# Mixing the last 64 tokens of two batches together, on the two column halves of the TensorE array

## Chip, cores and metric

The kernel runs on one core of one Trainium2 chip. The metric is device time in microseconds (us), lower is better; faster or slower needs 2%. PE is TensorE (PEld its weight loads), DVE is VectorE, ACT is ScalarE, POOL is GpSimd. "The page" is the printed profile of a run, and its chain is the work that ended last, followed back from the last instruction.

## The reference, cut

```python
# attention over pooled keys and values: 8 batches, 8 heads, 576 tokens, head width 64
k_p, v_p = means of k, v over groups of 8 tokens
x = softmax(q @ k_p^T / 8) @ v_p             # -> [8, 576, 512] float32
# residual MLP with a token mix
a1  = alpha1 * x + beta1
tok = einsum('ts,bsd->btd', w_tok, a1)       # mixes the 576 tokens of one batch
u   = x + lam * tok
ch  = relu((alpha2 * u + beta2) @ w_ch1) @ w_ch2
out = u + lam * ch
```

576 tokens are four chunks of 128 and a remainder of 64. The mix contracts 576 source tokens in five steps (four of 128, one of 64 or 65 with a bias row) for each chunk of target tokens.

## The kernel before, the parts concerned

The remainders of an even batch and of the odd one after it share one chunk of 128 rows: the even batch's tokens in rows 0 to 63, the odd batch's in rows 64 to 127. Each was mixed in its own batch's turn, with a full-width matmul of which half the rows were used.

```python
def chunk_of(b, c):
    key = (b, c) if c < 4 else (b - b % 2, 4)      # remainders of a pair: one chunk
    ...                                            # (cut) makes u (f32) and u_bf (bf16)

def mix_T(b, c, eng=nc.vector):
    key, s = chunk_of(b, c)
    p0, p1 = (0, P) if c < 4 else (64 * (b % 2), 64 * (b % 2) + 64)
    xs = xs_pool[b % 2]
    ps_tok = gp("ps_tok")
    t0 = P * c - 64 * (b % 2) if c == 4 else P * c
    for sc in range(5):
        kk, at = (P, sc) if sc < 4 else (P, 5) if b % 2 else (65, 4)
        nc.tensor.matmul(out=ps_tok, lhsT=wtT[0:kk, at, t0:t0 + P],          # L512
                         rhs=xs[0:kk, sc, :], start=(sc == 0), stop=(sc == 4))
    nc.vector.tensor_tensor(out=s["u"][p0:p1, :], in0=st1[b]["x"][p0:p1, c, :],
                            in1=ps_tok[p0:p1, 0:DM], op=ALU.add)             # L514
    eng.tensor_tensor(out=s["u_bf"][p0:p1, :], in0=s["u"][p0:p1, :],
                      in1=al2_bc[p0:p1, :], op=ALU.mult)                     # L516

def mix_uT(key):      # four PE transposes of u_bf (L527), one ACT copy into u_fm (L529)
    ...               # (cut)
```

The program is a list of pieces per block, sorted by a hand-chosen place. Block n runs the MLP of four chunks (`mlp_A` at places 0 to 15: matmuls L543 and a ReLU on ACT, L548; `mlp_B` at 16 to 31: matmuls L566) and in between the attention and the mix of batch n + 1.

```python
for c in range(5):
    at = 25.2 + 0.8 * c if late else 24.6 + (0.9 if b % 2 else 1.0) * c     # late: b == 1
    todo.append((at, lambda c=c: mix_T(b, c)))
    if c < 4 or b % 2:
        key = (b, c) if c < 4 else (b - 1, 4)
        todo.append((at + 2.2, lambda key=key: mix_uT(key)))
...                                                   # (cut)
if n == 0:
    todo.append((12.6, lambda: mix_T(0, 4)))
...                                                   # (cut) and, at the kernel's start:
keep_warm(4)                                          # four matmuls of constants, unused
```

The softmax here doesn't subtract the row's maximum and nothing guards it: scores larger than these inputs give would overflow.

Of the kernel before, what the change touches and what calls it, by code (L numbers as in the profile page):

```python
# [7 lines left out]
FP = mybir.dt.float32  # L8
F16 = mybir.dt.float16
BF = mybir.dt.bfloat16  # L10
AF = mybir.ActivationFunctionType
ALU = mybir.AluOpType
AX = mybir.AxisListType

P = 128
SPG = 72
DM = 512
# [6 lines left out]
def kernel(  # L24
# [18 lines left out]
    nc = tc.nc  # L43
    ctx.enter_context(tc.manual_schedule())
    B, H, S, D = q.shape

    const = ctx.enter_context(tc.tile_pool(name="const", bufs=1))
    work = ctx.enter_context(tc.tile_pool(name="work", bufs=1))
# [3 lines left out]
    def gp(name):  # L52
        return psA.tile([P, 512], FP, tag="gp", name=name)
# [10 lines left out]
    def keep_warm(count):  # L64

        ps = gp("ps_warm")
        for _ in range(count):
            nc.tensor.matmul(out=ps, lhsT=warm[:, 0:P], rhs=warm)


    st1 = {}

    def new_batch(b):
        st1[b] = {"qT": {}, "ET": [None] * H, "raw": [None] * 2, "q": [None] * 2,
                  "k": [None] * 2, "v": [None] * 2}
# [57 lines left out]
    def sum_k(b, u, eng):  # L133

        t = st1[b]["raw"][u][:, 1]
        bf = work.tile([P, 2, 2, D], BF, tag="k_bf", bufs=4, name="k_bf")
        for n in (4, 2):
            eng.tensor_tensor(out=t[:, :, 0:n], in0=t[:, :, 0:n], in1=t[:, :, n:2 * n], op=ALU.add)  # L138
        eng.tensor_tensor(out=bf, in0=t[:, :, 0:1].to_broadcast((P, 2, 2, D)),
                          in1=t[:, :, 1:2].to_broadcast((P, 2, 2, D)), op=ALU.add)  # L140
        st1[b]["k"][u] = bf
# [11 lines left out]
    al2_bc = const.tile([P, DM], FP, tag="al2_bc", name="al2_bc")  # L153
# [9 lines left out]
    start = const.tile([1, 2], FP, tag="start", name="start")  # L163
# [54 lines left out]
    def consts(shape, dt, name, count):  # L218
        return [const.tile(shape, dt, tag=f"{name}_{i}", name=f"{name}_{i}") for i in range(count)]
# [5 lines left out]
    xs_pool = consts([P, 5, DM], BF, "xs", 2)  # L225
# [3 lines left out]
    wtT = const.tile([P, 6, 640], BF, tag="wtT", name="wtT")  # L229

    def fill_v(i):
        nc.vector.memset(vp1_pool[i][0][0:64], 8.0)
        nc.vector.memset(vp1_pool[i][1][0:64], 0.0)
        nc.vector.memset(vp1_pool[i][1][64:128], 8.0)
        nc.vector.memset(vrem_pool[i][64:128], 0.0)
        nc.vector.memset(vrem_pool[i][0:64], 8.0)
# [27 lines left out]
    def broadcast(i):  # L264

        ps = psB.tile([P, DM], FP, tag="ch", bufs=2, name="ps_bc")
        nc.tensor.matmul(out=ps, lhsT=ones_row, rhs=vecs[0:1, i])
        return ps
# [226 lines left out]
    def chunk_of(b, c):  # L495
        key = (b, c) if c < 4 else (b - b % 2, 4)
        if key not in st2:
            st2[key] = {
                "u": work.tile([P, DM], FP, tag="u_sb", bufs=12, name="u_sb"),
                "u_bf": work.tile([P, DM], BF, tag="u_bf", bufs=4, name="u_bf"),  # L500
            }
        return key, st2[key]

    def mix_T(b, c, eng=nc.vector):
        key, s = chunk_of(b, c)
        p0, p1 = (0, P) if c < 4 else (64 * (b % 2), 64 * (b % 2) + 64)
        xs = xs_pool[b % 2]
        ps_tok = gp("ps_tok")
        t0 = P * c - 64 * (b % 2) if c == 4 else P * c
        for sc in range(5):  # L510
            kk, at = (P, sc) if sc < 4 else (P, 5) if b % 2 else (65, 4)
            nc.tensor.matmul(out=ps_tok, lhsT=wtT[0:kk, at, t0:t0 + P],  # L512
                             rhs=xs[0:kk, sc, :], start=(sc == 0), stop=(sc == 4))
        nc.vector.tensor_tensor(out=s["u"][p0:p1, :], in0=st1[b]["x"][p0:p1, c, :],  # L514
                                in1=ps_tok[p0:p1, 0:DM], op=ALU.add)
        eng.tensor_tensor(out=s["u_bf"][p0:p1, :], in0=s["u"][p0:p1, :],  # L516
                          in1=al2_bc[p0:p1, :], op=ALU.mult)

    def mix_uT(key):
        s = st2[key]  # L520
# [60 lines left out]


    new_batch(1)
    keep_warm(4)
    ps_lam = broadcast(0)
    nc.scalar.copy(out=lam_bc, in_=ps_lam)
    ps_lamal = broadcast(1)
# [73 lines left out]
        mlp_A(0, j, 256, 512)  # L661
    fill_v(1)

    ticks = const.tile([1, 2], FP, tag="ticks", name="ticks")

    def tick():
# [7 lines left out]
    def attention(b):  # L674


        late = b == 1
        todo = [(0.55 if late else -2.0, lambda: cast_rem(b, nc.gpsimd)),
                (10.0 if late else 6.0, lambda: sum_v_rem(b, nc.gpsimd)),
                (12.4 if late else 11.6, lambda: att_Vrem(b, nc.scalar.copy))]  # L680
        for u in range(2):
            copy = nc.scalar.copy if late and u else nc.gpsimd.tensor_copy
            q_at, f_at, k_at, v_at = (((0.5, 3.6, 5.4, 9.5), (6.0, 8.2, 10.0, 11.6))[u] if late else
                                      (None, 2.7 + 6.6 * u, 5.5 + 6.6 * u, 4.2 + 6.6 * u))
            k_from = q_at + 0.1 if late else -1.0 + u
            if late:
                todo.append((q_at, lambda u=u, copy=copy: cast_q(b, u, copy)))
            todo.append((k_from, lambda u=u: sum_k(b, u, nc.gpsimd)))
            todo.append((f_at, lambda u=u: att_F(b, u)))
            todo.append((f_at + 0.1, lambda u=u: att_Frem(b, (u,), nc.scalar.copy)))  # L690
            todo.append((k_at, lambda u=u: att_K(b, u, nc.vector.tensor_copy)))
            todo.append((v_at, lambda u=u: sum_v(b, u)))
            todo.append((v_at + (1.6 if late else 3.4 - u), lambda u=u: att_V(b, u, nc.scalar.copy)))
        for h in range(8):
            at = 13.3 + 1.0 * h if late else 13.1 + 1.0 * h
            todo.append((at, lambda h=h: att_S(b, h)))
            todo.append((at + 2.0, lambda h=h: att_AV(b, h)))
            if h % 2:
                eng = nc.vector if h == 7 else nc.gpsimd
                todo.append((at + 2.1, lambda h=h, eng=eng: att_X(b, h - 1, h + 1, eng)))  # L700
        todo.append((29.4, tick))
        if b > 1:
            todo.append((-2.1, pool_wait))
        for c in range(5):
            at = 25.2 + 0.8 * c if late else 24.6 + (0.9 if b % 2 else 1.0) * c
            todo.append((at, lambda c=c: mix_T(b, c)))
            if c < 4 or b % 2:
                key = (b, c) if c < 4 else (b - 1, 4)
                todo.append((at + 2.2, lambda key=key: mix_uT(key)))
        return todo  # L710

    for n in range(NBLK):
        todo = []
        for j in range(0 if n else 4, NJ):
            todo.append((j, lambda j=j: mlp_A(n, j)))
        for m in range(4):
            for part in range(4):
                at = 16 + (4 * m + part if n else 4 * part + m)
                todo.append((at, lambda m=m, part=part: mlp_B(n, m, part)))
        if n == 0:  # L720
            todo.append((12.6, lambda: mix_T(0, 4)))
            todo.append((13.0, lambda: row_of_xs(1, nc.gpsimd)))
            todo.append((9.4, lambda: setup_wtok(4, nc.scalar.copy)))
            todo.append((10.8, lambda: setup_rowsum(4)))
            todo.append((24.2, setup_wtok_odd))
            for g in range(1, 4):
                todo.append((4 * g - 0.8, lambda g=g: setup_bias(g)))
            for g in range(4):
                todo.append((3.0 + 1.5 * g, lambda g=g: load_w2(g)))
        if n == NBLK - 2:  # L730
            for j in range(NJ):
                todo.append((0.5 + 1.5 * j, lambda j=j: scale_w2(j)))
        b = n + 1
        if b < B:
            todo += attention(b)
            if b + 1 < B:
                new_batch(b + 1)
                for u in range(2):
                    todo.append((28.7 + 1.5 * u, lambda b=b, u=u: cast_q(b + 1, u, nc.scalar.copy)))
                    at = 21.0 + 0.2 * u if b == 1 else 0.4 + 1.0 * u  # L740
                    todo.append((at, lambda b=b, u=u: load_qk(b + 1, u)))
                    at = 23.0 + 0.2 * u if b == 1 else 5.8 + 6.6 * u
                    todo.append((at, lambda b=b, u=u: load_v(b + 1, u)))
                todo.append((21.1 if b == 1 else 0.9, lambda b=b: load_rem(b + 1)))
                todo.append((23.1 if b == 1 else 6.0, lambda b=b: load_v_rem(b + 1)))
        for _, do in sorted(todo, key=lambda x: x[0]):
            do()
# [30 lines left out]
```

## Time and profile before

| | before |
|---|---|
| median (first three runs) | 369.9 us (369.81 to 370.09) |
| span of the profiled run | 368.9 us |
| PE busy; share of the chain | 97%; 94% |
| first token mix to end of span | 368.95 - 25.60 = 343.35 us |

The prediction below shows the rows on PE and on the mix. One more view: ACT in block 0, from the timeline of the kernel before (columns: start, length in us, engine, line, operation, tiles, forms, count; in brackets the idle time before and who ended it).

```profile
39.57 0.69 ACT L548 ACTIVATE Hj<-ps_h,bias_cols 128x512 bf16<-128x512 f32 x1 [0.32 <-PE ps_h L543]
40.16 1.04 ACT L130 CAST q_bf<-qk_raw 128x1024 bf16<-128x1024 f32 x1
...
48.04 0.75 ACT L444 CAST vp<-ps_v 8x264 f16<-8x264 f32 x2
49.34 0.69 ACT L548 ACTIVATE Hj<-ps_h,bias_cols 128x512 bf16<-128x512 f32 x1 [0.55 <-PE ps_h L543]
```

ACT has one gap of 0.32 us before 39.57 and one of 0.55 us before 49.34. Two more, of 0.44 us before 45.81 and 0.21 us before 47.33, are the same in both kernels; otherwise, up to 55 us, it works without a break.

### The profile page before, as it was taken

What the parts mean: (1) busy time and instruction counts of PE and PEld (TensorE: products, weight loads), DVE (VectorE), ACT (ScalarE), POOL (GpSimd) and SP (SyncE); (2) the same over time, 40 slices, a digit from 0 to 9 for tenths busy, and PEclk for the clock granted to TensorE, in tenths of its full rate; (3) what the DMA queues carried; (4) which work ended last, traced back from release to release, by engine and by line L of the source; (5) the groups of instructions that cost most, each with busy time, mean ns of one, the idle gap of its engine ahead of it and who ended that gap; (6) DMA issues with size and microseconds to landing.
All of it is one profiled execution on the core that took longest, in us unless ns stands there. A gap on an engine that the chain in (4) does not pass through costs nothing.

```text
span 368.9 us, 6184 instructions
## 1 busy us (share of the span) xinstructions
PE 359.0 (97%) x2346; PEld 197.7 (54%) x2346; DVE 220.4 (60%) x437; ACT 213.9 (58%) x420; POOL 126.3 (34%) x182
## 2 busy tenths in 40 slices
PE   7799999999999999999999999999999999999995
PEld 2477555555545554555455555555455545544544
DVE  8765554883786358744876387727863687543011
ACT  3765984389527970698148923895279705712710
POOL 8766914072507231542227140905072410000000
PEclk9999999999999999999999999999999999999999
DMA  7999994039102901183107502470100002002002
GB/s 251 254 217 308 245 279 160 14 121 340 54 34 83 338 24 55 57 292 93 59 28 235 181 30 57 150 265 30 53 32 2 29 31 57 2 28 85 2 28 85
DMA packets 19575, 43.27 MB, mean 117 GB/s; under 512 B 2193, under 2 KB 4565, under 8 KB 19546
## 3 DMA queue, kind: packets, MB, share of 16 engines
q1 hardware_dynamic: 17488, 37.89, 30.8%
q0 software_dynamic: 1888, 4.86, 7.1%
q8 instruction: 18, 0.29, 0.3%
q10 hardware_dynamic: 170, 0.14, 0.2%
q14 instruction: 11, 0.09, 0.1%
HBM read 38.30 MB, written 9.44 MB: 129 GB/s over the span
## 4 chain that ended last, share of the span: by engine, by line
PE 94%; ACT 2%; DVE 2%; DMA 1%; ACTq 0%; issue 0%; DVEq 0%
PE ps_ch L566 34%; PE ps_h L543 33%; PE ps_tok L512 12%; PE ps_sc L453 5%; PE ps_av L470 2%; PE ps_uT L527 2%; PE ps_q L369 2%; DMA vecs<-in_moe_alpha_dram 1%; ACT Hj L548 1%; PE ps_w L288 1%; PE ps_av L473 1%; PE ps_rs L300 0%; PE ps_kp L401 0%; DVE qk_raw L138 0%; DVE xs L273 0%; ACT u_fm L529 0%
## 5 line engine op out<-in xcount | busy, mean ns | idle before, releaser
L543 PE MATMUL ps_h<-u_fm,w 128*128 128x512 bf16 (+1 forms) x592 | 134.7, 373 | 0.6 <-ACT u_fm L529 0.4
L566 PE MATMUL ps_ch<-w,Hj 128*128 128x512 bf16 x512 | 127.2, 379 | 0.0
L548 ACT ACTIVATE Hj<-ps_h,bias_cols 128x512 bf16<-128x512 f32 x144 | 97.1, 691 | 34.1 <-PE ps_h L543 33.6
L543 PEld LDWEIGHTS <-w 128*128 128x128 bf16 x592 | 64.1, 114 | 48.2 <-issue 0.6
L566 PEld LDWEIGHTS <-Hj 128*128 128x128 bf16 x592 | 55.6, 98 | 49.1 <-issue 0.2
L529 ACT COPY u_fm<-ps_uT 128x512 bf16<-128x512 bf16 x36 | 21.0, 588 | 80.4 <-PE ps_uT L527 80.4
L484 POOL TENSOR_TENSOR xs<-x_tm,lamal_bc 128x512 bf16<-128x512 f32 x24 | 30.5, 1272 | 81.2 <-DVE x_tm L477 81.2
L455 ACT ACTIVATE ET<-ps_sc 128x288 f16<-128x288 f32 (+1 forms) x128 | 51.6, 488 | 10.8 <-PE ps_sc L453 10.4
L512 PE MATMUL ps_tok<-xs,wtT 128*128 128x512 bf16 (+1 forms) x200 | 49.3, 379 | 0.0
L573 DVE TENSOR_TENSOR u_sb<-u_sb,ps_ch 128x512 f32<-128x512 f32 (+1 forms) x37 | 24.9, 672 | 24.9 <-PE ps_ch L566 23.8
L408 DVE CAST kpT<-ps_kp 64x288 bf16<-64x288 f32 x31 | 14.1, 455 | 40.6 <-PE ps_kp L404 40.4
L572 DVE TENSOR_TENSOR ps_ch<-lam_bc,ps_ch 128x512 f32<-128x512 f32 x32 | 22.2, 693 | 24.9 <-PE ps_ch L566 24.8
L514 DVE TENSOR_TENSOR u_sb<-x_tm,ps_tok 128x512 f32<-128x512 f32 (+1 forms) x40 | 27.4, 685 | 12.0 <-PE ps_tok L512 11.9
L477 DVE TENSOR_TENSOR x_tm<-ps_av,rec 128x320 f32<-128x320 f32 x64 | 31.5, 492 | 2.7
L475 DVE RECIPROCAL rec<-ps_av 128x5 f32<-128x5 f32 x64 | 12.4, 193 | 34.4 <-PE ps_av L473 34.2
L512 PEld LDWEIGHTS <-wtT 128*128 128x128 bf16 (+1 forms) x200 | 18.8, 98 | 23.3 <-DVE xs L484 1.9
L453 PE MATMUL ps_sc<-qT,kpT 128*128 128x288 bf16 (+1 forms) x128 | 29.1, 306 | 1.5 <-DVE kpT L408 1.5
L138 POOL TENSOR_TENSOR qk_raw<-qk_raw 128x512 f32<-128x512 f32 (+1 forms) x28 | 29.9, 1068 | 1.1
L516 DVE TENSOR_TENSOR u_bf<-u_sb,al_bc 128x512 bf16<-128x512 f32 (+1 forms) x39 | 27.3, 700 | 1.4
L671 POOL COPY ticks<-ticks 1x1 f32<-1x1 f32 x6 | 1.1, 178 | 73.4 <-DVE ticks L667 73.4
L416 DVE TENSOR_TENSOR v_u<-v_u 128x512 f32<-128x512 f32 (+1 forms) x30 | 24.7, 824 | 0.8
L470 PEld LDWEIGHTS <-ET 72*128 72x128 f16 (+1 forms) x256 | 17.0, 102 | 14.1 <-DVE vp L428 0.6
(115 smaller groups left out, 325.3 us busy)
## 6 DMA issues: line engine op xcount, KB each, us to landing
qk_raw<-in_q_dram SPq DMA_DIRECT2D x16, 512.0 KB, 8.2
qk_raw<-in_k_dram SPq DMA_DIRECT2D x16, 512.0 KB, 6.4
v_u<-in_v_dram SPq DMA_DIRECT2D x32, 256.0 KB, 7.4
out_dram<-u_sb SPq DMA_DIRECT2D x32, 256.0 KB, 2.2
w<-in_moe_w_ch_dram POOLq DMA_DIRECT2D x2, 1024.0 KB, 13.8
w<-in_moe_w_ch_dram POOLq DMA_DIRECT2D x4, 512.0 KB, 10.8
rem_raw<-in_q_dram SPq DMA_DIRECT2D x8, 128.0 KB, 4.7
rem_raw<-in_k_dram SPq DMA_DIRECT2D x8, 128.0 KB, 4.9
```

The source lines that it names most:

```text
L138: eng.tensor_tensor(out=t[:, :, 0:n], in0=t[:, :, 0:n], in1=t[:, :, n:2 * n], op=ALU.add)
L453: nc.tensor.matmul(out=ps_sc[0:n, 0:288], lhsT=kpT_pool[u][:, j, r, 72 * hh:72 * hh + n], rhs=st["qT"][u][:, h % 4, :])
L455: nc.scalar.activation(out=ET[0:n, 64 + j:64 + S + j:2], in_=ps_sc[0:n, 0:288], func=AF.Exp, bias=0.0, scale=1.0 / 64)
L477: nc.vector.tensor_tensor(out=x[:, :, dd:dd + D], in0=av[:, :, 0:64], in1=rec.unsqueeze(2).to_broadcast((P, 5, D)), op=ALU.mult)
L484: eng.tensor_tensor(out=xs[:, 0:4, cols], in0=x[:, 0:4, cols], in1=lamal_bc[:, cols].unsqueeze(1).to_broadcast((P, 4, D * (h1 - h0))), op= ...
L512: nc.tensor.matmul(out=ps_tok, lhsT=wtT[0:kk, at, t0:t0 + P], rhs=xs[0:kk, sc, :], start=(sc == 0), stop=(sc == 4))
L514: nc.vector.tensor_tensor(out=s["u"][p0:p1, :], in0=st1[b]["x"][p0:p1, c, :], in1=ps_tok[p0:p1, 0:DM], op=ALU.add)
L516: eng.tensor_tensor(out=s["u_bf"][p0:p1, :], in0=s["u"][p0:p1, :], in1=al2_bc[p0:p1, :], op=ALU.mult)
L543: nc.tensor.matmul(out=ps_h[:, t0:t1], lhsT=w1_of(cc, j), rhs=u_fm[n][:, cc, t0:t1], start=(cc == 0), stop=(cc == 3))
L548: nc.scalar.activation(out=t, in_=ps_h, func=AF.Relu, bias=bias_cols[:, j:j + 1], scale=1.0)
L566: nc.tensor.matmul(out=ps, lhsT=Hj[n, j][:, 128 * m:128 * m + 128], rhs=w2_of(n, j, cols), start=(j == 0), stop=(j == NJ - 1))
L573: nc.vector.tensor_tensor(out=u, in0=u, in1=ps, op=ALU.add)
```

## The change

The even batch's remainder is no longer mixed in its own turn. Its 64 rows of x are saved by an ACT copy (`save_rem`), and at the odd batch both remainders are mixed together: ten matmuls with 64 weight columns each, alternately into PSUM rows 0 to 63 and 64 to 127, that is, on the two column halves of the array (PSUM is the memory that TensorE writes; forms such as 128*64 in the views give rows and weight columns). The intent is that the two halves work at the same time. VectorE then does two adds of 64 rows and one multiply of 128. Beside it, one buffer of `k_bf` is given up for the space of `x_rem`, and the four warm-up matmuls at the start go.

```diff
@@ -133,7 +133,7 @@
     def sum_k(b, u, eng):
 
         t = st1[b]["raw"][u][:, 1]
-        bf = work.tile([P, 2, 2, D], BF, tag="k_bf", bufs=4, name="k_bf")
+        bf = work.tile([P, 2, 2, D], BF, tag="k_bf", bufs=3, name="k_bf")
         for n in (4, 2):
             eng.tensor_tensor(out=t[:, :, 0:n], in0=t[:, :, 0:n], in1=t[:, :, n:2 * n], op=ALU.add)
         eng.tensor_tensor(out=bf, in0=t[:, :, 0:1].to_broadcast((P, 2, 2, D)),
@@ -503,18 +503,32 @@
 
     def mix_T(b, c, eng=nc.vector):
         key, s = chunk_of(b, c)
-        p0, p1 = (0, P) if c < 4 else (64 * (b % 2), 64 * (b % 2) + 64)
         xs = xs_pool[b % 2]
         ps_tok = gp("ps_tok")
-        t0 = P * c - 64 * (b % 2) if c == 4 else P * c
         for sc in range(5):
             kk, at = (P, sc) if sc < 4 else (P, 5) if b % 2 else (65, 4)
-            nc.tensor.matmul(out=ps_tok, lhsT=wtT[0:kk, at, t0:t0 + P],
+            nc.tensor.matmul(out=ps_tok, lhsT=wtT[0:kk, at, P * c:P * c + P],
                              rhs=xs[0:kk, sc, :], start=(sc == 0), stop=(sc == 4))
-        nc.vector.tensor_tensor(out=s["u"][p0:p1, :], in0=st1[b]["x"][p0:p1, c, :],
-                                in1=ps_tok[p0:p1, 0:DM], op=ALU.add)
-        eng.tensor_tensor(out=s["u_bf"][p0:p1, :], in0=s["u"][p0:p1, :],
-                          in1=al2_bc[p0:p1, :], op=ALU.mult)
+        nc.vector.tensor_tensor(out=s["u"], in0=st1[b]["x"][:, c, :], in1=ps_tok, op=ALU.add)
+        eng.tensor_tensor(out=s["u_bf"], in0=s["u"], in1=al2_bc, op=ALU.mult)
+
+    def save_rem(b):
+
+        nc.scalar.copy(out=x_rem, in_=st1[b]["x"][0:64, 4, :])
+
+    def mix_T_rem(b):
+
+        key, s = chunk_of(b, 4)
+        ps_tok = gp("ps_tok")
+        for sc in range(5):
+            for i in range(2):
+                kk, at = (P, sc) if sc < 4 else (P, 5) if i else (65, 4)
+                nc.tensor.matmul(out=ps_tok[64 * i:64 * i + 64], lhsT=wtT[0:kk, at, 512:576],
+                                 rhs=xs_pool[i][0:kk, sc, :], start=(sc == 0), stop=(sc == 4))
+        for i, x in enumerate((x_rem, st1[b]["x"][64:128, 4, :])):
+            rows = slice(64 * i, 64 * i + 64)
+            nc.vector.tensor_tensor(out=s["u"][rows], in0=x, in1=ps_tok[rows], op=ALU.add)
+        nc.vector.tensor_tensor(out=s["u_bf"], in0=s["u"], in1=al2_bc, op=ALU.mult)
 
     def mix_uT(key):
         s = st2[key]
@@ -581,7 +595,6 @@
 
 
     new_batch(1)
-    keep_warm(4)
     ps_lam = broadcast(0)
     nc.scalar.copy(out=lam_bc, in_=ps_lam)
     ps_lamal = broadcast(1)
@@ -661,6 +674,7 @@
         mlp_A(0, j, 256, 512)
     fill_v(1)
 
+    x_rem = const.tile([64, DM], FP, tag="x_rem", name="x_rem")
     ticks = const.tile([1, 2], FP, tag="ticks", name="ticks")
 
     def tick():
@@ -701,9 +715,11 @@
         todo.append((29.4, tick))
         if b > 1:
             todo.append((-2.1, pool_wait))
-        for c in range(5):
+        if b % 2 == 0:
+            todo.append((23.4, lambda: save_rem(b)))
+        for c in range(4 + b % 2):
             at = 25.2 + 0.8 * c if late else 24.6 + (0.9 if b % 2 else 1.0) * c
-            todo.append((at, lambda c=c: mix_T(b, c)))
+            todo.append((at, lambda c=c: mix_T(b, c) if c < 4 else mix_T_rem(b)))
             if c < 4 or b % 2:
                 key = (b, c) if c < 4 else (b - 1, 4)
                 todo.append((at + 2.2, lambda key=key: mix_uT(key)))
@@ -718,7 +734,7 @@
                 at = 16 + (4 * m + part if n else 4 * part + m)
                 todo.append((at, lambda m=m, part=part: mlp_B(n, m, part)))
         if n == 0:
-            todo.append((12.6, lambda: mix_T(0, 4)))
+            todo.append((4.2, lambda: save_rem(0)))
             todo.append((13.0, lambda: row_of_xs(1, nc.gpsimd)))
             todo.append((9.4, lambda: setup_wtok(4, nc.scalar.copy)))
             todo.append((10.8, lambda: setup_rowsum(4)))
```

## The prediction

> **What bounds the kernel now.** I read the page first: busy shares, then the chain of work that ended last, then the groups. The page of the kernel before:
>
> ```profile
> PE 359.0 (97%) x2346; PEld 197.7 (54%) x2346; DVE 220.4 (60%) x437; ACT 213.9 (58%) x420; POOL 126.3 (34%) x182
> ...
> PE 94%; ACT 2%; DVE 2%; DMA 1%; ACTq 0%; issue 0%; DVEq 0%
> ...
> L512 PE MATMUL ps_tok<-xs,wtT 128*128 128x512 bf16 (+1 forms) x200 | 49.3, 379 | 0.0
> ```
>
> TensorE (PE) is busy nearly always and carries 94% of the chain, so PE time taken out comes off the end unless another engine takes its place. L512 is the token mix, the thing that is changed: 200 matmuls, never waited for by anything idle before them (0.0). The 379 ns in the row is one matmul's latency; what counts is the distance from start to start. The timeline of an odd batch (b = 3) shows it:
>
> ```profile
> 149.00 1.24 PE L512 MATMUL ps_tok<-xs,wtT 128*128 128x512 bf16 x5
> ...
> 150.28 0.69 DVE L514 TENSOR_TENSOR u_sb<-x_tm,ps_tok 64x512 f32<-64x512 f32 x1 [0.26 <-PE ps_tok L512]
> ...
> 151.01 0.69 DVE L516 TENSOR_TENSOR u_bf<-u_sb,al_bc 64x512 bf16<-64x512 f32 x1
> ...
> 152.26 0.39 PE L527 MATMUL ps_uT<-identity_bf,u_bf 128*128 128x128 bf16 x4
> ```
>
> Five matmuls last 1.24 us with the last one's latency of 0.38, so (1.24 - 0.38) / 4 = 0.215 us from start to start; the chain likewise books 1.08 us for each such five. The 64-token mix needs half of the array's columns but streams 512 elements all the same and pays the full 1.08 us. The result then goes through VectorE (L514, L516; 0.69 us each whether 64 or 128 rows), and the transpose L527 waits for it. Here u_bf is ready at 151.70 and the transpose starts at 152.26: about 0.5 us of slack.
>
> **What the Trainium skill says.** "TensorEngine Tiling (Array Packing)", Key Properties: tiles work independently, loads and matmuls of different tiles can go in parallel, and a change of tiling mode drains the engine. The trace before has no column tiling, so the parallel part is untested; it has one likely mode switch, the transposes of 64 rows at L288, seen below. Same page, Restrictions: column tiling turns fast weight load off. "TensorE: Matmul & The Clock Gate", LDWEIGHTS (loading the stationary operand): a load takes its column count over 1.2, so 64 columns are estimated at 53 ns and a pair at 107 ns. That fits under a stream of 215 ns, if it can be pulled ahead as it is now. Same page, Measured speedup vs the span model: three column tiles at 512 elements gave 2.38 times; I estimate that two give nearly two. No number here on five accumulating steps in a row.
>
> The switch, in two narrow windows of PE's timeline:
>
> ```profile
> 42.72 0.38 PE L543 MATMUL ps_h<-u_fm,w 128*128 128x512 bf16 x1
> 43.03 0.22 PE L288 MATMUL ps_w<-identity_bf,wt_bf 64*128 64x64 bf16 x1
> ```
> ```profile
> 43.15 0.22 PE L288 MATMUL ps_w<-identity_bf,wt_bf 64*128 64x64 bf16 x2
> 43.31 0.41 PE L543 MATMUL ps_h<-u_fm,w 128*128 128x512 bf16 x1
> ```
>
> Going in, 0.31 us from start to start where 0.215 is usual: 0.10 lost. Coming out, 0.16 from 43.15 where the loads of this group are about 0.03 apart: 0.13 lost. With the 0.02 by which the next matmul is late, a round trip costs 0.25 us. This is a row tiling, not a column one; I take it as the estimate.
>
> **The change part by part.**
>
> 1. *PE work.* Now each pair of batches has two five-matmul mixes of remainder tokens, 2 x 1.08 = 2.16 us. After it, ten 64-column matmuls, alternating between the two column halves. If halves run side by side: 5 x 0.216 = 1.08, plus 0.05 of stagger (the second load, above). Four pairs: 4 x (2.16 - 1.13) = 4.1 us off PE, all on the chain.
> 2. *Mode switches.* One round trip per pair: 4 x 0.25 = 1.0 us back.
> 3. *VectorE at the odd batch.* Before: one add and one multiply of 64 rows. After: two adds of 64 rows and one multiply of 128 rows, so one operation more, with 0.72 us from start to start, ahead of the transpose. At b = 3: the mix's first matmul starts at 149.10 instead of 149.00, its last at about 150.02 and ends at 150.40; adds and multiply run from 150.44 to 152.6. The transpose, moved by PE's own 0.28, would start at about 152.54: a wait of about 0.1, 0.12 with the semaphore. Three odd batches: 0.4 us. At b = 1 VectorE is already late (next view): the wait of 0.43 grows by 0.72 - 0.28, another 0.4 us. Together 0.8 us. What falls away at even batches (two operations, 1.4 us of VectorE) is off the chain and worth nothing.
> 4. *The saved rows.* A copy of 64x512 on ScalarE (ACT) per pair. From its casts of 1024 elements at 1.04 us and copies of 512 at 0.59 I take 0.57 us. For b = 2, 4, 6 it falls where ACT sits idle for 8 us before u_fm, so free. For b = 0 it falls after 37.9 us, where ACT has 0.32 us of idle time and is then itself the chain (casts and ReLUs 39.6 to 44.2): 0.57 - 0.32 = 0.25, say 0.3 us.
> 5. *The removed four warm-up matmuls.* They run from 2.19 to 4.08 at 0.43 us each, half speed, and the transposes at 7.72 still have 0.107 us distance, also half speed; only from 23.2 on are they fast. So they warmed nothing up. PE's first long product starts at 4.01 and might start a bit earlier, but the chain of the first 10 us runs through a DMA that lands at 4.79 and then VectorE until 10.76. Worth 0.
> 6. *k_bf with 3 buffers instead of 4.* At most two halves of a batch are in use at once; worth 0.
>
> The timeline of VectorE and of PE at b = 1:
>
> ```profile
> 72.62 0.69 DVE L514 TENSOR_TENSOR u_sb<-x_tm,ps_tok 64x512 f32<-64x512 f32 x1
> 73.35 0.69 DVE L516 TENSOR_TENSOR u_bf<-u_sb,al_bc 64x512 bf16<-64x512 f32 x1
> ```
> ```profile
> 74.09 0.40 PE L527 MATMUL ps_uT<-identity_bf,u_bf 128*128 128x128 bf16 x4
> ```
>
> L516 ends at 74.04 and the transpose starts 0.05 later: it waited for exactly this.
>
> Sum: -4.1 + 1.0 + 0.8 + 0.3 = -2.0 us. From 369.9 that gives 367.9; I say **368.0**.
>
> **The rivals.**
>
> *A: the halves don't run side by side.* If each ten stream one after another (loads wait for the half in flight, or two streams of 512 share one path), nothing is saved: 40 x 0.216 = 8.64 us as before, and the costs 1.0 + 0.8 + 0.3 stay: 372.0. For it: nothing in this trace shows two matmuls at once. Against: the skill states it and has measured packs. A milder form exposes the pair's loads, 107 ns in each of 20 steps: 2.1 us, 370.0.
>
> *B: every change of half drains*, so that each matmul costs its latency: 40 x 0.379 = 15.2 us, 6.5 more, with the rest 378. Against: the skill names the mode, not the tile, as what drains. I give it 3%.
>
> *C: ACT takes over at block 0.* The mix of b = 0 is removed at 47.2 us, where ACT is nearly always busy (from 49.3 to 55.4 without a gap). If PE's 1.08 us there only turns into waits for exponentials, up to 0.8 us more is lost: 368.8. For it: ACT's idle gaps there are 0.55 and 0.21 us. Against: the exponentials are ready 0.3 to 0.8 us before PE needs them.
>
> *D: no switch cost*, because a pulled-ahead load hides it, and no wait of the transpose: 369.9 - 4.1 + 0.3 = 366.1. The best case.
>
> **Range and chances.** Some 75% on side by side (366 to 369, depending on C and D), 20% on A in its two forms (370 to 372), the rest beyond. The range 366.2 to 370.6 holds about eight in ten. Two per cent are 7.4 us: even the whole of the removed PE time (4.3 us, 1.2%) does not reach it, and only B does on the other side. So faster 0.02, same 0.95, slower 0.03.
>
> **What would show it.** In the new trace the ten matmuls of 64 columns take about 1.5 us from first start to last end, starts of a pair close together and pairs 0.216 apart (A: 0.216 from each start to the next, 2.3 us; B: about 0.38). The matmul after them starts about 0.13 late, the first of them about 0.10. The transpose at the end of an odd block waits for L516's successor by about 0.1, at block 0 by about 0.9. ACT's new copies take about 0.57 us, and only the first one moves PE. The even blocks are 1.08 us shorter, the odd ones 0.4 longer. A start of the first products before 4 us that doesn't move the first score matmul (11.26) confirms step 5; a shift of the moment at which PE becomes fast would make it wrong, by up to a microsecond or so, and so would a transpose that is more than 0.2 us late in each odd block.

## The result, and the profile after

| | before | after |
|---|---|---|
| median | 370.0 us (369.81 to 370.92, 6 runs) | 368.05 us (367.07 to 368.53, 6 runs) |
| ratio | | 0.9937 (95% interval 0.9917 to 0.9958) |
| span of the profiled run | 368.9 | 366.7 |
| first token mix to end of span | 343.35 | 366.75 - 25.51 = 341.24 |

A ratio is the mean time of one kernel's runs over the mean of the other's in the same rounds, so it is not quite the ratio of the medians. The interval shows a gain of 0.4% to 0.8%.

The page of the changed kernel, busy shares and chain:

```profile
PE 352.8 (96%) x2300; PEld 194.5 (53%) x2342; DVE 212.3 (58%) x433; ACT 215.8 (59%) x424; POOL 126.5 (34%) x182
...
PE 87%; ACT 6%; DVE 3%; DMA 2%; issue 1%; SPq 1%; ACTq 0%
```

PE carries less of the chain (94% to 87%) and ACT more (2% to 6%). Do not read the fall of 6.2 us in PE's busy time as a gain: this trace lacks matmul records (2300 matmuls against 2342 weight loads), and the busy time of the two overlapped halves is counted once.

The timeline of PE at the odd batch b = 3, to be laid beside the lines at 149.00 to 152.26 of the prediction:

```profile
147.69 0.38 PE L580 MATMUL ps_ch<-w,Hj 128*128 128x512 bf16 x1
148.00 1.27 PE L526 MATMUL ps_tok<-xs,wtT 128*64 128x512 bf16 x10
149.20 0.40 PE L541 MATMUL ps_uT<-identity_bf,u_bf 128*128 128x128 bf16 x4
```

Ten matmuls of 512 elements take 1.27 us, where five took 1.24. The first starts 0.31 us after the last MLP matmul (0.216 is usual, so 0.095 for going in); the last starts at 148.89, and the transpose after it at 149.20, again 0.095 late. A narrow window, 147.99 to 148.20, shows the first pair: both matmuls have started (at 147.995 and 147.998, read one by one) before one stream of 0.216 us could be over.

```profile
148.00 0.41 PE L526 MATMUL ps_tok<-xs,wtT 128*64 128x512 bf16 x2
```

At b = 1 the transpose of the shared chunk now waits for VectorE (PE's timeline):

```profile
72.75 1.03 PE L580 MATMUL ps_ch<-w,Hj 128*128 128x512 bf16 x4
74.06 0.40 PE L541 MATMUL ps_uT<-identity_bf,u_bf 128*128 128x128 bf16 x4 [0.29 <-DVE u_bf L531]
```

Four MLP matmuls take 4 x 0.216 = 0.864 us, so the transpose could have started at 73.61. It starts at 74.06: 0.45 us of waiting. Before, by the same reckoning, 0.11.

ACT in block 0 of the changed kernel:

```profile
38.39 0.63 ACT L517 COPY x_rem<-x_tm 64x512 f32<-64x512 f32 x1
38.90 1.27 ACT L562 ACTIVATE Hj<-ps_h,bias_cols 128x512 bf16<-128x512 f32 x2
40.07 1.05 ACT L130 CAST q_bf<-qk_raw 128x1024 bf16<-128x1024 f32 x1
...
47.95 0.75 ACT L444 CAST vp<-ps_v 8x264 f16<-8x264 f32 x2
48.73 0.69 ACT L562 ACTIVATE Hj<-ps_h,bias_cols 128x512 bf16<-128x512 f32 x1
```

The copy (L517, 0.63 us) fills the gap of before: the cast at 40.16 is now at 40.07, 0.09 earlier, just as everything since the first mix (25.60, now 25.51). So it cost nothing. But the gap of 0.55 before 49.34 has also gone: from 47.2 to 54.8 us ACT works without a break and is now what PE waits for. The chain in the stretch 46.5 to 52 us (`--critical`), before and after, shows it:

```profile
by line: PE ps_h L543 63.3%; PE ps_tok L512 19.7%; PE ps_sc L453 16.4%; PE ps_av L470 2.2%; PE ps_v L442 2.2%; PE ps_v L424 1.0%; PE ps_av L473 0.5%; issue 0.3%
```
```profile
by line: ACT Hj L562 34.8%; ACT ET L455 15.1%; ACT vp L444 13.5%; PE ps_h L557 12.0%; PE ps_ch L580 11.8%; ACT vp L428 7.4%; PE ps_sc L453 5.1%; issue 3.8%; ACTq L562 0.3%
```

Where the time went, from the starts of matmuls in the two traces (how much earlier the changed kernel is):

| point | before | after | earlier by |
|---|---|---|---|
| first token mix | 25.60 | 25.51 | 0.09 |
| first `mlp_B` matmul of block 0 (even mix removed before it) | 51.99 | 51.39 | 0.60 |
| start of block 1 (shared mix of b = 1 before it) | 75.19 | 75.16 | 0.03 |
| start of block 2 (even mix of b = 2 removed) | 114.16 | 113.04 | 1.12 |
| start of block 3 (shared mix of b = 3) | 153.34 | 152.60 | 0.74 |
| start of block 5 | 231.50 | 230.03 | 1.47 |
| start of block 7 | 309.66 | 307.45 | 2.21 |
| end of span | 368.95 | 366.75 | 2.20 |

The first pair gained nothing beyond the start. Each of the other three gained about 0.73 us: some 1.1 in the even block, less some 0.37 in the odd one (predicted: 1.08 and 0.4).

### The profile page after: what moved, and what is told of

Its sections match the earlier page's. It is cut to its first block, busy times and chain, and to the rows that moved or that the text cites. A ratio compares the mean times of both kernels' runs of the same rounds, so it can differ in the third digit from the quotient of the medians.

```text
span 366.7 us, 6128 instructions
## 1 busy us (share of the span) xinstructions
PE 352.8 (96%) x2300; PEld 194.5 (53%) x2342; DVE 212.3 (58%) x433; ACT 215.8 (59%) x424; POOL 126.5 (34%) x182
## 4 chain that ended last, share of the span: by engine, by line
PE 87%; ACT 6%; DVE 3%; DMA 2%; issue 1%; SPq 1%; ACTq 0%
PE ps_ch L580 33%; PE ps_h L557 30%; PE ps_tok L510 9%; PE ps_sc L453 4%; ACT Hj L562 3%; PE ps_av L470 2%; PE ps_uT L541 2%; DMA qk_raw<-in_k_dram 2%; PE ps_q L369 1%; PE ps_tok L526 1%; ACT qT L373 1%; PE ps_w L288 1%; SPq L84 1%; PE ps_av L473 1%; PE ps_kp L401 1%
## 5 line engine op out<-in xcount | busy, mean ns | idle before, releaser
L580 PE MATMUL ps_ch<-w,Hj 128*128 128x512 bf16 x495 | 124.0, 379 | 1.2 <-issue 0.3
L510 PE MATMUL ps_tok<-xs,wtT 128*128 128x512 bf16 (+1 forms) x155 | 38.7, 379 | 0.2
L512 DVE TENSOR_TENSOR u_sb<-x_tm,ps_tok 128x512 f32<-128x512 f32 x32 | 21.9, 685 | 9.8 <-PE ps_tok L510 9.3
L510 PEld LDWEIGHTS <-wtT 128*128 128x128 bf16 (+1 forms) x160 | 15.0, 98 | 19.1 <-DVE xs L484 2.0
L513 DVE TENSOR_TENSOR u_bf<-u_sb,al_bc 128x512 bf16<-128x512 f32 x31 | 21.8, 704 | 1.1
L416 DVE TENSOR_TENSOR v_u<-v_u 128x512 f32<-128x512 f32 (+1 forms) x30 | 20.8, 693 | 0.8
```

Source lines behind the costliest of these rows:

```text
L510: nc.tensor.matmul(out=ps_tok, lhsT=wtT[0:kk, at, P * c:P * c + P], rhs=xs[0:kk, sc, :], start=(sc == 0), stop=(sc == 4))
L580: nc.tensor.matmul(out=ps, lhsT=Hj[n, j][:, 128 * m:128 * m + 128], rhs=w2_of(n, j, cols), start=(j == 0), stop=(j == NJ - 1))
```

## The experiments

Eleven runs were made, all with a correct result; each is compared with the kernel before in the same rounds. In the last column is the time from the first token mix to the end of the span, which leaves the varying start out; with it, the two profiles of the changed kernel agree within 0.1 us (the kernel before has one profile).

| run | median us (before) | ratio, 95% interval | first mix to end |
|---|---|---|---|
| before (profile) | | 1 | 343.35 |
| changed kernel | 368.05 (370.0) | 0.9917 to 0.9958 | 341.24 |
| a0_after_again | 367.43 (369.93) | 0.9924 to 0.9948 | 341.16 |
| e1_halves_in_turn | 368.74 (369.93) | 0.9940 to 0.9976 | 341.81 |
| e5_warm_kept | 367.64 (369.93) | 0.9932 to 0.9960 | 341.16 |
| e6_later_uT | 367.42 (369.93) | 0.9917 to 0.9946 | 340.61 |
| e2_full_width | 370.52 (370.22) | 0.9993 to 1.0032 | 343.86 |
| e3_switch_x5 | 374.03 (370.22) | 1.0091 to 1.0124 | 347.49 |
| e4_same_work_after | 370.37 (370.22) | 0.9988 to 1.0024 | 343.89 |
| e7_vrem_dve | 367.54 (370.22) | 0.9912 to 0.9946 | 340.69 |
| e8_both | 366.72 (370.39) | 0.9870 to 0.9910 | 339.76 |
| e10_same_half | 371.36 (370.39) | 1.0006 to 1.0043 | 344.63 |
| e9_save_twice | 367.48 (370.39) | 0.9906 to 0.9950 | 341.78 |

### The yardstick

No edit.

> The changed kernel once more, unaltered, as the yardstick for the other runs of this call and to see how far two of its runs and traces lie apart. Theory: 368.0, between 367.0 and 368.6 as in its six runs; from the first token mix to the end of the span the same length as in its first trace (366.7 - 25.5 = 341.2) within 0.2, because what varies is the start.

Measured 367.43, and 341.16 from first mix to end, 0.08 from the first trace. The span is 1.16 us shorter than in the first trace (365.59 against 366.75), all but 0.08 of it before the first mix, which starts at 24.43 instead of 25.51. The 128-wide transposes stop being slow (0.107 us apart) after 21.2 us here and after 23.4 us in the first trace; in the kernel before after 23.5. That is the moment from which the traces' record of the granted clock stays at full speed: 21.13, 23.59 and 23.53. Over all thirteen traces it lies between 20.50 and 23.59, and the start of the first mix goes with it (correlation 0.90): up to 21.2 us, the mix starts at 23.93 to 24.80 (six traces); from 22.7 us on, at 25.16 to 25.80 (five); the two between start at 24.71 and 25.30. No run moved it on purpose, so a cause is not shown.

### Is it the overlap of two halves?

First way: both remainders at the odd batch as in the change, but each with 128 columns.

```diff
-        for sc in range(5):
-            for i in range(2):
+        ps_two = ps_tok, gp("ps_tok2")
+        for i in range(2):
+            for sc in range(5):
                 kk, at = ...
-                nc.tensor.matmul(out=ps_tok[64 * i:64 * i + 64], lhsT=wtT[0:kk, at, 512:576],
+                t0 = 512 - 64 * i
+                nc.tensor.matmul(out=ps_two[i], lhsT=wtT[0:kk, at, t0:t0 + P],
                 ...                                  # (cut) and the adds read ps_two[i][rows]
```

> Both remainder mixes at the odd batch as in the changed kernel, but each with all 128 columns as in the kernel before: no halves, no mode switch, same copies, same VectorE work. Theory (the gain is the overlap of the two halves): per pair 2.16 us for 1.10 + 0.20 of switches, four times 0.86 more, 371.4, and at the mixes no gap of 0.1 us before and after. Rival (the gain comes from moving the even batch's mix out of its place and from fewer VectorE operations): 368 to 369.

Measured 370.52 against 370.22 of before: all of the gain is gone. From the timeline of PE at b = 3 (one of the ten records is missing):

```profile
147.48 2.33 PE L528 MATMUL ps_tok<-xs,wtT 128*128 128x512 bf16 x9
149.64 0.39 PE L543 MATMUL ps_uT<-identity_bf,u_bf 128*128 128x128 bf16 x4
```

From the mix to the next work 2.16 us, no gap on either side. The change needs 147.90 to 149.20 for that, 1.30 us: 0.86 less, as expected. Four times 0.86 is 3.44, less the 0.81 us of waits at the transposes that vanish here, gives 2.63; measured from first mix to end, 343.86 - 341.20 = 2.66 (341.20 is the mean of the changed kernel's two traces). (The expectation of 371.4 had left those waits out.) So moving the mixes and saving VectorE operations is worth nothing by itself.

Second way: the same ten instructions, but one half's five steps first.

```diff
-        for sc in range(5):
-            for i in range(2):
+        for i in range(2):
+            for sc in range(5):
```

> All five steps of the even batch's half first, then all five of the odd batch's half: the same ten instructions in another order. Theory (two halves run at once only where neighbouring matmuls go to different halves): five in a row on one half stream one after another, so each mix takes 10 x 0.216 = 2.16 us for 1.10, four times 1.06 us more: 372.3. Rival (the gain comes from 64 columns being cheaper as such, or from where the mix stands in the order): 368.0, unchanged.

Measured 368.74; the theory asked for 372.3. **This expectation failed**, and the trace says how. Three windows of PE's timeline at b = 3: the whole mix; what had started by 148.45; and, from a window just before 148.88, the even batch's fifth and last step, known by its 65 rows.

```profile
147.61 1.51 PE L526 MATMUL ps_tok<-xs,wtT 128*64 128x512 bf16 x10
```
```profile
147.61 1.08 PE L526 MATMUL ps_tok<-xs,wtT 128*64 128x512 bf16 x7
```
```profile
148.50 0.62 PE L526 MATMUL ps_tok<-xs,wtT 65*64 65x512 bf16 x3
```

In the program the 65-row matmul is the fifth of the ten. By its start at 148.50 seven had started, not four: three of the odd batch's half, which stand after it in the program, had overtaken it. Read one by one and sorted by their steps of about 0.216 us, the even half's five start at 147.610, 147.850, 148.065, 148.281 and 148.497, the odd half's at 147.855, 148.095, 148.311, 148.527 and 148.743. The compiler did not reorder them: the kernel sets its own order (`tc.manual_schedule()`), and the program built from it once more has the 65-row matmul fifth of the ten. The halves run as two streams, each in its own order, and the later one lags by one step. The cost is one more step of 0.24 us per mix, 0.97 in all; the waits at the transposes shrink by some 0.3 (at b = 1 from 0.45 to 0.21), and 0.65 us is left: 341.81 - 341.16.

Third way, after this miss: both batches on the same half, into two PSUM banks.

```diff
+        ps_two = ps_tok, gp("ps_tok2")
-                nc.tensor.matmul(out=ps_tok[64 * i:64 * i + 64], lhsT=wtT[0:kk, at, 512:576],
+                nc.tensor.matmul(out=ps_two[i][0:64], lhsT=wtT[0:kk, at, 512:576],
                 ...                                  # (cut) and the adds read ps_two[i][0:64]
```

> Both batches' 64 columns on the same half of the array, into two banks, in the order of the changed kernel; the right result, since VectorE reads the second bank's lower rows. The run with the halves in turn did not serialise, so this one takes the overlap away in another way. Theory (the gain is two different halves at work at once): 10 x 0.216 = 2.16 us per mix, four times 1.06 more, with no wait left at the transposes 0.7 less: 370.9. Rival (64 columns stream faster by themselves, or the front end lets any two accumulations overlap): 367.5.

Measured 371.36. PE at b = 3:

```profile
148.37 2.35 PE L527 MATMUL ps_tok<-xs,wtT 128*64 128x512 bf16 x10
150.66 0.40 PE L542 MATMUL ps_uT<-identity_bf,u_bf 128*128 128x128 bf16 x4
```

2.35 us for the same ten shapes. A 64-column matmul streams its 512 elements no faster than a full one, and two groups on one half do not overlap. Two different halves are needed, and e1 shows that they are enough in the other order too.

### What does a change of the array's tiling cost?

Both with the later transposes of e6, so that no wait hides anything. In e3 a full-width matmul stands between the five pairs; in e4 the same four stand behind them.

```diff
+        ps_x = gp("ps_warm")
         for sc in range(5):
             for i in range(2):
                 ...                                  # the two halves
+            if sc < 4:                               # e4: after the loop, four times
+                nc.tensor.matmul(out=ps_x, lhsT=warm[:, 0:P], rhs=warm)
```

> With the later transposes; a full-width matmul of 512 put between the five pairs of each mix, so four mode round trips more per mix, 16 in all. Against the next run, which has the same 16 matmuls behind the mix. Theory (a round trip costs 0.20 us whatever stands between): 367.2 + 16 x 0.216 = 370.7, and 16 x 0.20 = 3.2 more: 373.9. Rival (the two gaps are not switches but the start of an accumulation, or a load that came late once): 370.7, the same as the next.

> With the later transposes; four full-width matmuls behind each mix: one round trip per mix as in the change. Both theories: 367.2 + 16 x 0.216 = 370.7.

Measured 374.03 against 370.37: 3.66 us for 16 more round trips. First mix to end gives 347.49 - 343.89 = 3.60, or 0.225 us each. In the timeline of e3:

```profile
148.48 0.41 PE L527 MATMUL ps_tok<-xs,wtT 128*64 128x512 bf16 x2
148.82 0.39 PE L530 MATMUL ps_warm<-warm 128*128 128x512 bf16 x1
149.14 0.41 PE L527 MATMUL ps_tok<-xs,wtT 128*64 128x512 bf16 x2
```

Pair to full width 0.34 and full width to pair 0.32 us, where 0.216 is the stream: about 0.12 and 0.10 lost. The rival is out. What the loss consists of stays open: at each of these switches the first weight load starts only 2 to 4 ns before its matmul, while inside a mix of the changed kernel it starts some 0.21 us before (148.022 for 148.235). An array that has to run empty and a load that cannot be pulled ahead look the same here.

### The removed warm-up

One line put back, ahead of the first product:

```diff
     new_batch(1)
+    keep_warm(4)
     ps_lam = broadcast(0)
```

> The changed kernel with the four warm-up matmuls at the start put back. Theory (they were off the chain and warmed nothing): within 0.3 us of the changed kernel, 368.0, and the moment at which 128-wide transposes go from 0.107 to under 0.06 us of distance stays near 23.5 us. Rival (their removal gave the change a good part of its gain, through an earlier start of the products): 0.5 to 1 us slower, 368.5 to 369.

Measured 367.64 against 367.43; the intervals of the two overlap, so no effect is seen. (The same 341.16 says nothing here, since it leaves the start out.) The transposes stop being slow after 20.9 us and not near 23.5 as expected, but that moment varies without any edit. The first token mix starts at 24.68 and, in the kernel before, 25.60 with the warm-up; at 23.93 to 25.80 without it.

### PE waiting for VectorE's one operation more

```diff
-                todo.append((at + 2.2, lambda key=key: mix_uT(key)))
+                todo.append((at + 2.2 if c < 4 else 31.5, lambda key=key: mix_uT(key)))
```

> The changed kernel with the transposes of the remainder chunk moved behind the block's last matmuls (it is used two blocks later). Theory (TensorE waits for VectorE's one operation more: 0.45 us at batch 1, 0.12 at each of the three others): the waits vanish, 0.8 us less: 367.2. Rival (those gaps are the cost of the transpose itself or would have turned up elsewhere): 368.0.

By the median (367.42 against 367.43) this shows nothing, so the runs alone leave it open. In the trace the waits are gone (b = 1: eight MLP matmuls in a row, then the transpose without a gap), and from block 0's first `mlp_B` matmul to the end it takes 365.41 - 50.98 = 314.43 us against 365.59 - 50.29 = 315.30, 0.87 less. But this one profile lost 0.3 us in the part before, whose code is unaltered. Its trace shows where: a transfer landed late, POOL waited 1.28 us for it (0 to 0.94 in the other traces), and PE's weights from `k_bf` came late in turn.

```profile
33.50 0.40 POOL L121 CAST rem_q<-rem_raw 128x256 bf16<-128x256 f32 x1 [1.28 <-DMA rem_raw<-in_q_dram]
...
37.86 0.11 PEld L401 LDWEIGHTS <-k_bf 128*128 128x128 bf16 x2 [0.61 <-POOL k_bf L139]
```

e8 repeats the edit without this delay.

### Where block 0 lost half of its gain

```diff
-                (12.4 if late else 11.6, lambda: att_Vrem(b, nc.scalar.copy))]
+                (12.4 if late else 11.6, lambda: att_Vrem(b, nc.vector.tensor_copy if late else nc.scalar.copy))]
```

> The changed kernel with the two casts of the pooled remainder of v at batch 1 (0.75 us on ScalarE, at 48 us) moved to VectorE, in block 0 alone. Theory (of the 1.08 us that the removed even mix gives back at 47 us, 0.57 is lost because ScalarE, with ReLUs, casts and exponentials in a row, is then the chain there): up to 0.57 us comes back, 367.5. Rival (it is lost elsewhere, to the copy of the saved rows or to TensorE's order): 368.0.

By the median 367.54, at the expected value, but other runs of the changed kernel also reach it. The trace is clear: from the first mix to block 0's first `mlp_B` matmul 50.61 - 25.30 = 25.31 us, against 25.88 in the changed kernel and 26.39 in the kernel before. The full 1.08 us of the removed mix now arrives. The chain from 46.5 to 52 us is PE's again, and ACT has an idle time of 0.24 us that it had not (the 0.20 before 47.03 was there in the changed kernel too, as 0.21). ACT's timeline, then the chain:

```profile
47.03 0.69 ACT L562 ACTIVATE Hj<-ps_h,bias_cols 128x512 bf16<-128x512 f32 x1 [0.20 <-PE ps_h L557]
47.96 0.69 ACT L562 ACTIVATE Hj<-ps_h,bias_cols 128x512 bf16<-128x512 f32 x1 [0.24 <-PE ps_h L557]
```
```profile
by line: PE ps_h L557 55.0%; PE ps_sc L453 23.8%; PE ps_ch L580 15.7%; PE ps_av L470 4.4%; PE ps_v L442 2.2%; issue 1.2%; PE ps_av L473 1.1%; PE ps_v L424 1.0%
```

The opposite edit, the copy of the saved rows made twice:

```diff
             todo.append((4.2, lambda: save_rem(0)))
+            todo.append((4.2, lambda: save_rem(0)))
```

> The copy of the saved rows in block 0 made twice. Theory (the first one only filled a gap of ScalarE of about half a microsecond before it becomes the chain; the gap is now gone): the second one costs its 0.46 to 0.6 us, from the first token mix to the end 341.2 + 0.5 = 341.7. Rival (ScalarE still has slack there, since the change lost nothing at this place): 341.2.

341.78 from first mix to end, or 0.6 us more than the changed kernel, the length of the copy. All of it is lost before the first `mlp_B` matmul (26.49 us from the first mix instead of 25.88), where PE now waits for the cast behind the copies:

```profile
40.24 0.45 PEld L369 LDWEIGHTS <-q_bf 128*128 128x128 bf16 x8 [0.57 <-ACT q_bf L130]
```

The first copy was free because a gap was there; the second is on the chain. The median (367.48) does not show this; in the profiled run (367.5) the first mix came at 23.93, half a microsecond earlier than in any other trace.

### Both together

The two one-line edits of e6 and e7 in one kernel, as shown there.

> Later transposes of the remainder chunk and the casts of v's remainder on VectorE together. Theory: from the first token mix to the end 341.2 in the changed kernel, less 0.9 (waits of the transposes) and 0.55 (ScalarE in block 0): 339.7; the whole run, whose start varies by a microsecond, near 366.2 against 367.5 for the changed kernel, the fastest here. Rival (the two relieve the same slack, so the gains do not add): 340.3 and 366.7.

Median 366.72, ratio 0.987 to 0.991: the fastest kernel here, by 1.1% against before. From first mix to end it takes 339.76, the sum (341.2 - 0.9 - 0.55). The part before `mlp_B` is that of e7 (25.30) and the part after it that of e6 (314.46), so both readings stand. Between the changed kernel's interval and this one's there is no overlap.

## Why the prediction was right, step by step

The predicted 368.0 met the measured 368.05. That the two agree to 0.05 us is luck: the same kernel's median in the next call was 367.43, and the misses of the steps below (0.1, 0.2, 0.1 and 0.27 us) largely cancel. Steps 1 and 2 were right for a reason that the runs showed, step 3 in its sum only, and step 4 named the wrong place.

1. **PE work, predicted -4.1 us; traced -4.2.** The ten matmuls take PE from 147.995 to 149.10, 1.11 us, where I had 1.13. The stagger between the two of a pair is 3 ns, not one weight load. One sum in the prediction is wrong by its own figures: from first start to last end it gives 149.10 to 150.40, or 1.3 us, in one place and 1.5 us in another; 1.27 was measured. Rivals A (no overlap, 372.0) and B (a drain at each change of half) fall with the ten in 1.27 us; e2 and e10 show what no overlap costs.
2. **Switches, predicted 1.0; traced 0.8.** 0.19 us per round trip at b = 3, 0.225 in e3. The row-tiled transposes of the kernel before were a usable stand-in for a column-tiled mix. They were misread, though: the line at 43.15 stands for two matmuls (x2), the second starting at 43.187, so that coming out loses 0.09 and not 0.13, and a round trip 0.21 and not 0.25, which is nearer to what was measured. Rival D, no cost, falls.
3. **Waits of the transposes, predicted 0.8; traced 0.70.** At b = 3 the transpose could start at 150.52 + 0.86 = 151.38 and starts at 151.50, the 0.12 that was predicted. At b = 1 the wait grew by 0.34 (predicted: 0.4). The starting figure there was misread: the 0.43 in the prediction is idle time of the weight-load row; by the reckoning of PE's own starts the wait before was 0.11, and so the wait after is 0.45 and not the 0.9 that was to be seen. The increase was computed from VectorE's operations and survived that. e6 and e8 show that it can be taken away.
4. **ACT in block 0, predicted 0.3; traced 0.57, at another place.** Here the step failed. The prediction charged the copy of the saved rows, 0.57 minus a gap of 0.32. The copy was free (e9 shows that only a second one costs). The loss came 9 us later, where the removed mix let PE run into ACT: that is rival C, which I had left out of the sum because the exponentials seemed ready 0.3 to 0.8 us early. That slack was of the old timing. e7 gives the 0.56 us back.
5. **Warm-up and buffer, predicted 0.** For the warm-up e5 agrees in the total. The sign that the prediction named did not come: the first products start at 2.7 to 3.0 us instead of 4.01, but the first score matmul moved as well, from 11.26 in both traces with the warm-up to between 10.26 and 11.28 in the eleven without. Nothing of that is seen at the first token mix (correlation 0.17 over the thirteen traces). The buffer of `k_bf` was not tried alone; no wait of its writers for a free buffer is seen.

Sum of the traced terms: -4.2 + 0.8 + 0.7 + 0.57 = -2.1; measured from first mix to end, 341.24 - 343.35 = -2.11. So half of the PE time that was freed came off the end; the other half was paid for switches, for one VectorE operation in PE's way, and for ACT in one block.

## What to carry to other kernels

Two half-width accumulations on the two column halves of the array cost little more than one (one step of 0.24 us more when the program issues them one after the other); the price is a switch of about 0.2 us per visit, so collect such work and visit seldom. When PE time is taken out of a balanced stage, check who has gaps there: a gap on another engine is the room that the gain has (here a gap of 0.55 us let 0.51 of 1.08 us through), and the slack that you read before the change is not the slack after it. When a kernel's start varies by more than the effect, compare trace intervals that leave it out, and support them with a run that adds the effects up.

## What the Trainium skill lacked or had wrong

- "TensorE: Matmul & The Clock Gate", section The mechanism, says that matmuls stay in the order of the program, in start and end. That does not hold across column halves: in e1 three matmuls of the odd batch's half started before the even half's fifth, which stands before them (148.497 against 147.855, 148.095 and 148.311). The last one issued was still the last to start there. Whether a semaphore on the last-issued matmul would then be safe was not tested.
- "TensorEngine Tiling (Array Packing)", Key Properties, says that changing the tiling mode drains the engine, but gives no cost: 0.19 us per round trip at b = 3, 0.225 over 16 of them (about 0.10 in, 0.12 out, between streams of 512). That it is a drain is not shown by these runs.
- No page has a figure for accumulating column pairs: five steps of two halves ran in 1.11 us, at 0.216 us per pair. The loads of 64 columns last 106 to 110 ns in the trace, twice the 53 ns that the prediction worked out from "TensorE: Matmul & The Clock Gate", LDWEIGHTS, and longer than the 95 to 99 ns of the mix's loads of 128 columns; inside a mix they were hidden under the streams.
- "TensorE: Matmul & The Clock Gate", The HAM clock gate, gives about 3.4 us of sustained work to reach full speed. Here PE worked from 2.19 to 8.96 us without a break in the kernel before (3.8 us of it on matmuls with one row), and the 128-wide transposes at the end of that stretch were still 0.107 us apart. Full speed came to stay only at 20.50 to 23.59 us in the thirteen traces. In seven of them the record of the clock shows one spell of 3.41 us at full speed before that, beginning between 13.67 and 16.15 us, and then 3.41 us at half (in a0, from 14.31, 17.72 and 21.13 us on). What sets these moments stays open.
